# Four PSUM banks in turn for the spectral sums of an adaLN block, forward and backward

## The chip, the cores and the metric

The kernel runs on one NeuronCore of one Trainium2 chip. Its time is the device time in microseconds from launch to end. Three runs of the kernel before gave 1523.6, 1515.2 and 1520.55 us, so the median is 1520.55 us. One further execution was profiled. It took 1518.75 us, and from its first to its last instruction (the span) 1516.6 us; every duration below is from that execution.

A matmul writes its sums into PSUM, a small memory with eight banks. Each bank holds 512 fp32 values per partition, and another engine must copy ("evacuate") a bank to SBUF before it can be written anew. Which bank a group of matmuls gets therefore decides which evacuation it has to wait for.

## The reference

A transformer block with a spectral mixing layer (A) and an MLP (B) is computed, with the gradients of all its inputs but one constant; S = 2048 tokens, D = 1024, F = 3584, in bf16:

```python
def _A_ref(x, w_r, w_i):
    X = rfft2(x.astype(float32), axes=(-2, -1))
    X = X * (w_r + 1j * w_i)
    return irfft2(X, s=(S, D), axes=(-2, -1)).astype(bfloat16)

def _B_ref(x, w1, b1, w2, b2):
    h = gelu(layernorm(x) @ w1 + b1)
    return h @ w2 + b2

sa, ca, ga, sb, cb, gb = split(silu(c) @ w_mod, 6)
h = layernorm(x) * (1 + ca) + sa
x = x + ga * _A_ref(h, w_r, w_i)
h = layernorm(x) * (1 + cb) + sb
x = x + gb * _B_ref(h, w1, b1, w2, b2)
# returned: x, and the vector-Jacobian product of this block for grad_out
```

## The kernel before

The 2-D transforms are done as matmuls with cosine and sine matrices. The input is folded first (sums and differences of mirrored rows and columns), which leaves four parity classes: cosine even and odd, sine even and odd (`CE, CO, SE, SO` = 0, 1, 2, 3). One function, `spectral_core`, does the whole of it twice: forward on the normalised x, and backward on the gradient. Its steps are:

1. `s_fwd`, once for each class: the transform along the tokens. Eight groups of four matmuls 128x512 (`pu`, L470), into `ps_s` banks.
2. `pair(n, par, m)`, eight times (n = 4·par + m): the transform along the features. For t = 0 the cosine class and for t = 1 the sine class of one parity; for each t two banks `pcs[0]` and `pcs[1]`, and into each of them two groups of two matmuls 128x256 (L503). Both banks are then copied into `cs`, with `nc.any` in the forward pass (the scheduler takes ACT or DVE; the line is L641) and on ACT in the backward pass (L644). Then a chain of DVE operations follows (all through the helper `tt`, L172): `Pt` from `cs`, the products `qa` and `qb` with the spectral weights `ws`, and two rows of `R`. Forward, `Pt` is stored to `d_P`; backward it is loaded again into `pf` and gives the weights' gradients, which are stored by SP and by POOL (L549, L550). The weights of the next pair are loaded by `pair_load` (SP L488 and POOL L489, which gathers mirrored rows).
3. `s_inv`, once for each class: the inverse along the tokens from `R`, eight groups of four matmuls 128x512 (`pv`, L563), in `ps_s` banks. `CE` and `SE` run ahead of pair 6, `CO` and `SO` after pair 7.
4. The inverse along the features: for each of four blocks of tokens (i = 0 to 3) and each class, two groups of four matmuls 128x256 (`po`, L628), each copied into `ct` by ACT or DVE (L631). `consume` then works on the block: `consume_fwd` unfolds it, adds the residual, normalises it and stores it; `consume_bwd` goes on to the layer norm's gradient and the output.

PSUM is shared out by three helpers over one pool. `ps_s` has two banks in turn (tag s: `pu`, `pv`, and in the backward pass `accCA`, an accumulator held from the first block of step 4 to the last), `ps_d` two (tag d: `pcs`, `po`, and other accumulators) and `ps_f` four (tag f: the large products). A tile asked for under a tag gets the tag's next bank in turn and waits until that bank's last reader is done.

PE always has other work beside these steps. Forward, it is `pp` (L678, the gradient of the output through w2; w2's tiles are loaded by SP as `wt`, and the results stored by POOL as `d_ph`). Backward, it is `gw2acc` (L1114, the gradient of w2): `beside_bwd` puts four groups of 16 matmuls 128x512 into each pair, and their evacuations `gwo` (L1119) are stored by POOL (L1121); the operand tiles `hh` are loaded by SP (L1139, two for each pair). In step 4 `consume_bwd` places more of it, and then `gw1acc` (L1181, the gradient of w1), whose remainder runs alone at the end. Between the passes lie the MLP's products: `pz` (L795) with the GELU on ACT and DVE (L798 to L806), `pbo` (L836), and `pg` (L1020).

The order on each engine isn't the order of the text. A scheduler places every instruction when its operands and its tile's bank come free in the scheduler's own model, and takes those under `tc.high_priority()` (the evacuations) first. So a change of banks can move instructions on all engines.

Of the kernel before, what the change touches and what calls it, by code (L numbers as in the profile page):

```python
# [35 lines left out]
def kernel(  # L36
# [39 lines left out]
    def ps_d(name):  # L76
        return psum.tile([P, 512], FP32, tag="d", name=name)
# [84 lines left out]
    def w_plus(w, par, m):  # L162
        return bass.AP(tensor=w.tensor, offset=w.offset + (256 * m + par) * DF, ap=[[2 * DF, P], [1, DF]])

    def w_idx(par, m):
        return bass.IndirectOffsetOnAxis(ap=widx[:, 4 * par + m:4 * par + m + 1], axis=0)
# [4 lines left out]
    def tt(out, a, b, op):  # L171
        return nc.vector.tensor_tensor(out=out, in0=a, in1=b, op=op)  # L172
# [303 lines left out]
    def spectral_core(fwd, fb, sms, em, css, pt, evac_u, evac_c, evac_v, consume, o4tag, pfs=None, fill=lambda n: None, mid=lambda: None, beside=lambda n: None):  # L476
# [16 lines left out]
        def pair(n, par, m):  # L493
            ws = ws2[:, n % 2]
            cs = css[n % 2]
            for t in range(2):
                cl = par + 2 * t
                pcs = [ps_d("pcs"), ps_d("pcs")]
                for dc in range(4):
                    po = pcs[0 if dc < 2 else 1]  # L500
                    st = dc % 2 if dc < 2 else 3 - dc
                    for h in range(2):
                        nc.tensor.matmul(po[:, st * 256:(st + 1) * 256], lhsT=Us[cl][:, 2 * dc + h, m * P:(m + 1) * P],  # L503
                                         rhs=em[:, 2 * dc + h, :], start=(h == 0), stop=(h == 1))
                c0 = 0 if t == 0 else PW
                s0 = 1 + (PW if t == 0 else 0)
                for k, o in ((0, c0), (1, s0)):
                    with tc.high_priority():
                        evac_c(cs[:, t, o:o + 512].rearrange("p (w s) -> p s w", s=2), pcs[k].rearrange("p (s w) -> p s w", s=2))
            Pt = Pt2[:, n % 2]  # L510
            cv = cs.rearrange("p t (x w) -> p t x w", w=PW)
            tt(Pt[:, 2:0:-1, :], cv[:, 0], cv[:, 1], ALU.add)
            tt(Pt[:, 0:4:3, :], cv[:, 0], cv[:, 1], ALU.subtract)
            sp_m = par == 0 and m == 0
            if sp_m:
                nc.vector.tensor_copy(out=Pt[0:1, 0:2, :], in_=cv[0:1, 0])
                nc.vector.tensor_scalar(out=Pt[0:1, 2, :], in0=cv[0:1, 1, 0], scalar1=-1.0, scalar2=None, op0=ALU.mult)
                nc.vector.tensor_copy(out=Pt[0:1, 3, :], in_=cv[0:1, 1, 1])
            Pv = Pt.rearrange("p (s r) w -> p s r w", r=2)[:, :, :, 0:DF]
            if fwd:  # L520
                nc.gpsimd.dma_start(out=d_P[n], in_=Pt.rearrange("p a w -> p (a w)"))
            qa = qa2[:, n % 2]
            qb = qb2[:, 0]

            def bc(x):
                a = ws[:, x, :, 0:DF]
                return bass.AP(tensor=a.tensor, offset=a.offset, ap=[a.ap[0], a.ap[1], [0, 2], a.ap[2]])

            tt(qa[:, :, :, 0:DF], Pv, bc(0), ALU.mult)
            tt(qb[:, :, :, 0:DF], Pv, bc(1), ALU.mult)  # L530
            tt(qa[:, :, 0, 0:DF], qa[:, :, 0, 0:DF], qb[:, :, 1, 0:DF], ALU.add if fwd else ALU.subtract)
            tt(qa[:, :, 1, 0:DF], qa[:, :, 1, 0:DF], qb[:, :, 0, 0:DF], ALU.subtract if fwd else ALU.add)
            rc = par * 4 + m
            rs = (par + 2) * 4 + m
            tt(R[:, rc, :, 0:DF], qa[:, 0, :, 0:DF], qa[:, 1, :, 0:DF], ALU.add)
            r_in[0] = tt(R[:, rs, :, 0:DF], qa[:, 0, :, 0:DF], qa[:, 1, :, 0:DF], ALU.subtract)
            if sp_m:
                nc.vector.tensor_copy(out=R[0:1, rc, :, 0:DF], in_=qa[0:1, 0, :, 0:DF])
                nc.vector.tensor_copy(out=R[0:1, rs, :, 0:DF], in_=qa[0:1, 1, :, 0:DF])
            if not fwd:  # L540
                pf = pfs[n % 2]
                m1 = qb2[:, 0]
                m2 = qb2[:, 1]
                tt(m1[:, :, :, 0:DF], Pv, pf[:, :, :, 0:DF], ALU.mult)
                tt(m2[:, :, :, 0:DF], Pv, pf[:, :, ::-1, 0:DF], ALU.mult)
                tt(pf[:, 0, :, 0:DF], m1[:, :, 0, 0:DF], m1[:, :, 1, 0:DF], ALU.add)
                tt(pf[:, 1, :, 0:DF], m2[:, :, 0, 0:DF], m2[:, :, 1, 0:DF], ALU.subtract)
                for x, w in ((0, out_2), (1, out_3)):
                    nc.sync.dma_start(out=w_plus(w, par, m), in_=pf[:, x, 0, 0:DF])  # L549
                    nc.gpsimd.indirect_dma_start(out=w, out_offset=w_idx(par, m), in_=pf[:, x, 1, 0:DF], in_offset=None)  # L550
# [38 lines left out]
        for par in range(2):  # L589
            for m in range(4):  # L590
                if par == 1 and m == 2:
                    s_inv(CE, smis[0])
                    s_inv(SE, smis[0])
                pair(par * 4 + m, par, m)
                if par * 4 + m < 7:
                    pair_load(par * 4 + m + 1)
                beside(par * 4 + m)
                if par == 0 and m == 0:
                    load_smi()
                if par == 0 and m > 0:  # L600
                    v = 0 if fwd else 1
                    if m == 1:
                        gm = reg.tile([P, 12, 256], BF16, name="gm", tag="gm")
                        for cl in (CO, SO):
                            with tc.issue_after(ld_in[0].ins):
                                nc.sync.dma_start(out=gm[:, 2 * cl:2 * cl + 2, :], in_=d_E[:, v, 2 * cl:2 * cl + 2, :])
                    else:
                        cl = (CE, SE)[m - 2]
                        for h in range(2):
                            with tc.issue_after(ld_in[0].ins):  # L610
                                nc.sync.dma_start_transpose(out=gm[:, 2 * cl:2 * cl + 2, h * P:(h + 1) * P],
                                                            in_=d_E[:, v, 2 * cl + h, :])
# [6 lines left out]
        for i in range(4):  # L619
            o4 = ct[:, 3 * (i % 2)]  # L620
            for cl in range(4):
                for hh_ in range(2):
                    po = ps_d("po")
                    for d2 in range(2):
                        dc = 2 * hh_ + d2
                        for h in range(2):
                            gi = 2 * dc + h + (4 if (dc >= 2 and cl >= 2) else 0)
                            nc.tensor.matmul(po[:, d2 * 256:(d2 + 1) * 256], lhsT=Vs[cl][:, 2 * dc + h, i * P:(i + 1) * P],  # L628
                                             rhs=gm[:, gi, :], start=(h == 0), stop=(h == 1))
                    with tc.high_priority():  # L630
                        nc.any.tensor_copy(out=o4[:, cl, hh_ * 512:(hh_ + 1) * 512], in_=po[:])  # L631
            consume(i, o4, ct[:, 1 + i % 2], ct[:, 2 - i % 2], xts[i % 2])
# [87 lines left out]
    def consume_fwd(i, o4, tmp, tmp2, x4):  # L720
# [13 lines left out]
        nc.sync.dma_start(out=chunk_rows(d_n3, i), in_=tmp)  # L734

    spectral_core(True, fbuf, (smA, smB), em1[:, 1], [css[:, 0], css[:, 1]], new_pair_temps(PXT[2:6]),
                  act_copy, act_copy, act_copy, consume_fwd, "fr")

# [262 lines left out]
    for b in range(NB):  # L1001
# [26 lines left out]
        for i in range(4):  # L1028
            t = 4 * b + i
# [9 lines left out]
        for i in range(4):  # L1039
            t = 4 * b + i  # L1040
# [175 lines left out]
    def beside_bwd(n):  # L1216
        for k in range(4):
            fill(1)
            if 3 - k < (1, 2, 2, 2, 2, 2, 3, 3)[n]:
                with tc.issue_after(hh_in[0].ins):  # L1220
                    next(rows34)

    spectral_core(False, fbuf2, (smA2, smB2), em2, [css2[:, 0], css2[:, 1]],
                  new_pair_temps(["t0", "t1", "t2", "t3"]), act_copy, s_copy, act_copy, consume_bwd, "fr", pfs, fill, mid_bwd, beside_bwd)

# [55 lines left out]
```

## Time and profile before

| What | us |
|---|---|
| Median of three runs | 1520.55 (1515.2 to 1523.6) |
| Profiled execution | 1518.75 |
| Its span, first to last instruction | 1516.6 |
| PE busy in the span | 1413.6 (93%) |
| DVE busy | 1070.0 (71%) |
| ACT busy | 724.6 (48%) |
| Mean granted TensorE clock | 0.980 |

The stages of that span, from the busy time by window:

| Stage, us from the start | length | PE busy | DVE busy | ACT busy | clock |
|---|---|---|---|---|---|
| modulation, w2 transposes, first pp: 0 to 95 | 95 | 67.9 | 71.7 | 61.4 | 0.93 |
| forward fold and `s_fwd`: 95 to 153 | 58 | 57.1 | 28.4 | 33.4 | 1.00 |
| forward pairs: 153 to 220 | 67 | 59.1 | 53.1 | 37.3 | 0.95 |
| forward inverse: 220 to 276 | 56 | 55.0 | 41.3 | 35.8 | 1.00 |
| rest of pp: 276 to 349 | 73 | 70.8 | 67.0 | 45.4 | 1.00 |
| MLP forward: 349 to 780 | 431 | 414.3 | 325.2 | 269.1 | 1.00 |
| MLP backward, first gw2: 780 to 1067 | 287 | 263.2 | 203.4 | 82.8 | 0.96 |
| backward `s_fwd`: 1067 to 1096 | 29 | 28.8 | 0.7 | 19.6 | 1.00 |
| backward pairs: 1096 to 1252 | 156 | 144.4 | 104.7 | 52.2 | 0.97 |
| backward inverse: 1252 to 1380 | 128 | 123.3 | 100.3 | 60.7 | 1.00 |
| rest of gw1: 1380 to 1517 | 137 | 129.8 | 74.4 | 26.9 | 0.99 |

How to read such a profile: an engine's busy time says how much work it has, not whether it sets the time. That is told by what ends the idle time of each engine (the waits), and by the chain of waits, which goes back from the last instruction to whatever released it. "Clock" is the share of full speed that the chip granted to TensorE in that stretch.

The durations of the operations that the change touches, from the groups by tile: a `pcs` or `po` matmul lasts 272 ns, and since matmuls overlap, a group of four takes some 0.43 us; an evacuation of `pcs` takes 738 ns on ACT and 736 on DVE in the forward pass, and 741 on ACT in the backward pass; one of `po` 585 ns on ACT and 692 on DVE. There are 256 `pcs` and 256 `po` matmuls, and 64 evacuations of each.

### The profile page before, as it was taken

How to read it: one execution, taken by the hardware profiler on the slowest of the kernel's cores; microseconds unless marked ns; L12 is line 12 of the kernel's file. 1: busy time of each engine (PE TensorE's matmuls, PEld its weight loads, DVE VectorE, ACT ScalarE, POOL GpSimd, SP SyncE). 2: the span in 40 equal slices, each digit the busy share in tenths (PEclk: the TensorE clock that was granted, in tenths of full speed). 3: DMA queues.
4: the chain of work that ended last, by engine and by line, in shares of the span. 5: the costliest groups of instructions: out<-in, count | busy, mean ns of one | idle time of the engine just before them, and what ended most of it. 6: DMA issues, size and time to landing. Idle time of an engine off the chain costs nothing.

```text
span 1516.6 us, 18226 instructions
## 1 busy us (share of the span) xinstructions
PE 1413.6 (93%) x6702; PEld 654.1 (43%) x6835; DVE 1070.0 (71%) x1575; ACT 724.6 (48%) x959; POOL 370.1 (24%) x427
## 2 busy tenths in 40 slices
PE   5899899999899999999889999969999899999998
PEld 2444445444344444444334444424444444444443
DVE  5883767897799887877313877958075775998633
ACT  4765556758787765666011423322622344443211
POOL 5710621210112122211112101321033331232333
PEclk8999999999999999999999999979999999999999
DMA  9882564999787776899956246398388976856994
GB/s 337 260 222 70 153 181 153 277 241 323 236 251 238 231 239 230 242 291 261 326 190 220 99 150 222 124 225 195 82 202 212 238 227 177 225 170 164 274 244 151
DMA packets 358168, 324.27 MB, mean 214 GB/s; under 512 B 209191, under 2 KB 300861, under 8 KB 357824
## 3 DMA queue, kind: packets, MB, share of 16 engines
q1 hardware_dynamic: 324192, 207.71, 51.3%
q0 software_dynamic: 33888, 115.41, 22.8%
q8 instruction: 53, 0.87, 0.2%
q14 instruction: 35, 0.29, 0.1%
HBM read 164.15 MB, written 109.10 MB: 180 GB/s over the span
## 4 chain that ended last, share of the span: by engine, by line
PE 49%; DVE 20%; issue 10%; DMA 10%; ACT 6%; POOL 4%; SPq 1%; POOLq 0%; ACTq 0%; DVEq 0%
PE pbo L836 10%; PE pz L795 10%; PE gw2acc L1114 9%; PE pg L1020 5%; PE gw1acc L1181 4%; PE pv L563 3%; DVE ct L172 3%; PE pu L470 3%; PE pp L678 2%; DVE got L919 2%; DVE fbuf L172 2%; PE po L628 1%; DVE gn3a L924 1%; DMA gB<-in_grad_out_dram 1%; ACT ct L460 1%
## 5 line engine op out<-in xcount | busy, mean ns | idle before, releaser
L678 PE MATMUL pp<-gBoT,wt 128*128 128x512 bf16 x876 | 198.4, 379 | 5.6 <-DMA wt<-in_B_w_dram 1.9
L1020 PE MATMUL pg<-w1T,gzr 128*128 128x512 bf16 x876 | 195.3, 381 | 1.5 <-issue 0.7
L1181 PE MATMUL gw1acc<-gzh,n3n 128*128 128x512 bf16 x876 | 194.7, 379 | 0.9
L795 PEld LDWEIGHTS <-w 128*128 128x128 bf16 x896 | 87.7, 98 | 111.3 <-issue 7.9
L1020 PEld LDWEIGHTS <-gzr 128*128 128x128 bf16 x896 | 87.2, 98 | 109.4 <-issue 7.2
L678 PEld LDWEIGHTS <-wt 128*128 128x128 bf16 x896 | 87.4, 98 | 106.3 <-issue 3.7
L1181 PEld LDWEIGHTS <-n3n 128*128 128x128 bf16 x896 | 87.4, 98 | 104.1 <-issue 1.3
L795 PE MATMUL pz<-n3Ta,w 128*128 128x512 bf16 x437 | 99.5, 383 | 5.0 <-ACT gt L798 4.2
L1114 PE MATMUL gw2acc<-gB,hhsA 128*128 128x512 bf16 x437 | 100.7, 383 | 1.2 <-DMA hhsA<-d_hh 0.4
L1119 ACT CAST gwo<-gw2acc 128x512 bf16<-128x512 f32 x54 | 30.8, 584 | 146.7 <-PE gw2acc L1114 94.8
L795 PE MATMUL pz<-n3Tb,w 128*128 128x512 bf16 x439 | 98.4, 379 | 0.5
L836 PEld LDWEIGHTS <-hhA 128*128 128x128 bf16 x608 | 59.0, 98 | 75.2 <-issue 5.2
L798 ACT ACTIVATE gt<-pz,b_col 128x512 bf16<-128x512 f32 x112 | 73.0, 683 | 34.4 <-PE pz L795 32.3
L804 ACT ACTIVATE gt<-gt 128x2048 bf16<-128x2048 bf16 x28 | 53.5, 1910 | 67.5 <-DVE gt L172 67.5
L172 DVE TENSOR_TENSOR gt<-gt,gt 128x2048 bf16<-128x2048 bf16 x56 | 68.5, 1223 | 21.6 <-ACT gt L806 20.9
L1185 ACT CAST gwo<-gw1acc 128x512 bf16<-128x512 f32 x49 | 28.3, 582 | 104.9 <-PE gw1acc L1181 91.5
L172 DVE TENSOR_TENSOR ct<-ct 128x2048 bf16<-128x2048 bf16 x64 | 76.0, 1219 | 3.2 <-ACT ct L631 1.9
L1114 PE MATMUL gw2acc<-gB,hht 128*128 128x512 bf16 x251 | 59.4, 396 | 14.3 <-DMA hht<-d_hh 10.3
L1114 PEld LDWEIGHTS <-hhsA 128*128 128x128 bf16 x448 | 44.1, 99 | 52.6 <-issue 2.7
L800 ACT ACTIVATE gt<-gt 128x2048 bf16<-128x2048 bf16 x28 | 53.4, 1907 | 0.6
L806 ACT ACTIVATE gt<-gt 128x2048 bf16<-128x2048 bf16 x28 | 53.4, 1907 | 0.5
L958 DVE CUSTOM_DVE_ANT_0 otl<-otl 128x1024 bf16<-128x1024 bf16 x16 | 19.1, 1223 | 43.6 <-DMA otl<-in_w_mod_dram 35.6
(313 smaller groups left out, 2521.1 us busy)
## 6 DMA issues: line engine op xcount, KB each, us to landing
gzr<-d_gz SPq DMA_DIRECT2D x28, 512.0 KB
wblk<-in_w_mod_dram SPq DMA_DIRECT2D x12, 1024.0 KB
d_ph<-pho POOLq DMA_DIRECT2D x21, 512.0 KB
out_dram<-otl POOLq DMA_DIRECT2D x40, 256.0 KB
d_hh<-hhA POOLq DMA_DIRECT2D x19, 512.0 KB
w2sD<-in_B_w_dram SPq DMA_DIRECT2D x14, 512.0 KB
hhC<-d_ph SPq DMA_DIRECT2D x14, 512.0 KB
w2sA<-d_ph SPq DMA_DIRECT2D x14, 512.0 KB
```

What stands on the lines that cost most here:

```text
L172: return nc.vector.tensor_tensor(out=out, in0=a, in1=b, op=op)
L470: last_pu[0] = nc.tensor.matmul(pu[:], lhsT=fb[:, i, cl, c8 * P:(c8 + 1) * P], rhs=sm[:, i, :], start=(i == 0), stop=(i == 3))
L678: last_pe[0] = nc.tensor.matmul(pp[:], lhsT=wt[:, fg % 2, cch, k * P:(k + 1) * P], rhs=gBoT[j][:, cch, :], start=(cch == 0), stop=(cch == ...
L795: last_pe[0] = nc.tensor.matmul(pz[:], lhsT=w1s[g][:, cch, k * P:(k + 1) * P], rhs=n3T[:, cch, :], start=(cch == 0), stop=(cch == NDC - 1))
L798: nc.scalar.activation(out=zb[:, k, :], in_=pz[:], func=ACT.Identity, bias=b1_col[:, fc:fc + 1], scale=1.0)
L800: nc.scalar.activation(out=av, in_=zb, func=ACT.Square)
L804: nc.scalar.activation(out=sg, in_=bv, func=ACT.Sigmoid, scale=2.0 * GK)
L806: nc.scalar.activation(out=bv, in_=bv, func=ACT.Sigmoid, scale=-2.0 * GK)
L836: last_pe[0] = nc.tensor.matmul(pbs[i][:], lhsT=hh[:, k, i * P:(i + 1) * P], rhs=wp[:, k, :], start=False, stop=(g == 6 and k == 3))
L1020: nc.tensor.matmul(pgs[i][:], lhsT=gzt[g][:, k, i * P:(i + 1) * P], rhs=w1Ts[g][:, k, h * KH:(h + 1) * KH], start=(g == 0 and k == 0), sto ...
L1114: nc.tensor.matmul(acc[:], lhsT=hh_s[hh_o[fc]][:, t, :], rhs=gBs[t // 4][:, t % 4, h * KH:(h + 1) * KH], start=(t == 0), stop=(t == NT - 1))
L1181: nc.tensor.matmul(acc[:], lhsT=n3ns[t // 4][:, t % 4, cch * P:(cch + 1) * P], rhs=gz2[t // 8][:, t % 8, :], start=(t == 0), stop=(t == NT ...
```

## The change

Two lines are changed, both in `spectral_core`, so both passes are concerned. In `pair`, the two sums of t = 0 stay in the d banks, and the two of t = 1 take the s banks. In step 4, the first half of each class (`hh_` = 0) stays in a d bank and the second takes an s bank. The matmuls, the copies and all sizes are as before; so are the other users of the banks.

```diff
             for t in range(2):
                 cl = par + 2 * t
-                pcs = [ps_d("pcs"), ps_d("pcs")]
+                pcs = [(ps_d, ps_s)[t]("pcs") for _ in range(2)]
                 for dc in range(4):
                     po = pcs[0 if dc < 2 else 1]
...
             for cl in range(4):
                 for hh_ in range(2):
-                    po = ps_d("po")
+                    po = (ps_d, ps_s)[hh_]("po")
                     for d2 in range(2):
                         dc = 2 * hh_ + d2
```

## The prediction

> **What bounds the kernel now.** I read the page first (busy shares, slices, chain), then the waits of the two spectral passes, the busy time by stage, and the timelines of PE and ACT at the one place that decides.
>
> ```profile
> PE 1413.6 (93%) x6702; PEld 654.1 (43%) x6835; DVE 1070.0 (71%) x1575; ACT 724.6 (48%) x959; POOL 370.1 (24%) x427
> PEclk8999999999999999999999999979999999999999
> PE 49%; DVE 20%; issue 10%; DMA 10%; ACT 6%; POOL 4%; SPq 1%; POOLq 0%; ACTq 0%; DVEq 0%
> ```
>
> PE is busy for 1413.6 of 1516.6 us, so everything that a PSUM change could win lies in 103 us of PE idleness, in the clock lost after idle stretches, and only where PE sets the pace. The chain of waits is half PE and otherwise DVE, DMA and issue: in some stages PE waits because data are late, and banks don't help there. The waits from 1096 to 1380 us, the whole backward pass of the changed lines, name the PSUM waits:
>
> ```profile
> PE pcs L503 <- ACT cs01b L644: 8.6, 8, 2.5
> PE po L628 <- ACT ct L631: 3.8, 3, 2.7
> PE pv L563 <- ACT V L641: 1.6, 1, 1.6
> PE gw2acc L1114 <- DMA hhsA<-d_hh: 0.4, 1, 0.4
> ```
>
> So 8.6 us are lost at the second half of the sums (t=1) until ACT has read the first half's two banks, in eight waits: five of 0.22 to 0.27 us and three long ones, 2.51 us at 1163.81, 2.31 at 1184.30, 2.50 at 1236.36. The inverse sums lose 3.8 us. The forward pass (150 to 280 us) shows far less of it:
>
> ```profile
> PE pv L563 <- DVE R L172: 5.4, 1, 5.4
> ...
> PE pcs L503 <- ACT cs L641: 1.3, 6, 0.4
> ```
>
> There PE's one large wait is for DVE's product R, which no bank shortens. By stage (window: length, busy time of PE, PEld, DVE, ACT, POOL, then the granted clock, DMA share, GB/s), pairs 4, 5, 6 and 7 of the backward pass:
>
> ```profile
> 1160.00:1180.70 20.70, 17.69 (x80) 8.17 (x80) 11.16 (x17) 4.75 (x8) 7.03 (x9) 0.92 0.96 206
> 1180.70:1201.00 20.30, 17.57 (x80) 8.19 (x81) 12.15 (x18) 4.76 (x8) 6.75 (x8) 0.92 0.98 222
> ...
> 1216.50:1232.60 16.10, 15.77 (x79) 7.81 (x80) 10.35 (x14) 6.76 (x9) 4.12 (x5) 1.00 0.78 245
> 1232.60:1252.50 19.90, 17.35 (x80) 8.42 (x80) 15.60 (x24) 7.55 (x13) 5.34 (x8) 0.91 0.82 240
> ```
>
> A pair with a long wait takes 19.9 to 20.7 us, one without 16.1: each wait of some 2.5 us costs about 4, since the granted clock after it is lower (0.91 to 0.92 over the pair). PE at pair 7, and ACT just then:
>
> ```profile
> 1232.61 1.04 PE L503 MATMUL pcs<-empf,U 128*128 128x256 bf16 x8
> 1233.48 0.38 PE L1114 MATMUL gw2acc<-gB,otl 128*128 128x512 bf16 x1
> 1236.36 1.72 PE L503 MATMUL pcs<-empf,U 128*128 128x256 bf16 x8 [2.50 <-ACT cs01b L644]
> ```
>
> ```profile
> 1232.99 1.24 ACT L460 ACTIVATE xt<-xt,stats 128x1024 bf16<-128x1024 bf16 x1
> 1234.13 1.55 ACT L1119 CAST gwo<-gw2acc 128x512 bf16<-128x512 f32 x3
> 1235.55 1.36 ACT L644 CAST cs01b<-pcs 128x512 bf16<-128x512 f32 x2
> ```
>
> Eight matmuls take 1.72 us after the wait instead of 1.04. ACT reads the sums at 1235.55 only because three gw2 casts and a scale stand ahead; those are late because the stores of gwo are (ACT waits 39.2 us for them between 1160 and 1253).
>
> **The change, part by part.** Instruction counts stay; one evacuation moves from ACT to DVE. The t=1 sums get the two class-sum banks (tag s), the inverse sums alternate between d and s. By the built order of both programs, the four sums of a pair now run back to back (16 groups in a row for the forward pairs 0 to 3), and the gw2acc or pp matmul that stood between the halves follows.
>
> *Backward pairs 0 to 5 (0 us).* Their waits are 0.22+0.27+0.27+0.27+2.51+2.31 = 5.85 us, with the clock some (20.70−16.10)+(20.30−16.10)+1.03 = 9.8 us. But pairs 3 to 5 are held by the transfers: SP's loop of loads for one pair has a period of about 20 us (1140.96, 1159.97, 1180.45, 1200.68), the DMA share is 0.96 to 0.98, PE already waits 0.43 us for a tile of hhsA at 1173.83 that lands just then, and at 1204.42 PE waits 1.59 us for ACT, itself behind a gwo store until 1202.81. A PE that arrives earlier waits longer there. Price if that cover is gone: 9.8 us.
>
> *Backward pairs 6 and 7 (−4.5 us).* Here tiles are ahead. Pair 6's wait gives 0.2. In pair 7 four groups (4×0.43=1.7 us) and 64 gw2acc matmuls (64×0.216=13.85) from 1232.6 end at 1248.2 instead of 1252.5, where pv needs R. DVE's last R ended at 1247.3 after a start set by the fourth evacuation (1238.85); ACT would have that about 0.4 earlier: R at 1246.9, in time. So −4.3, of which 2.5 is the wait and the rest clock and issue. DVE then idles 16.59 us until po, so the consume chain moves with it.
>
> [...]
>
> *Backward inverse sums (0 us).* Waits now: 0.91+0.15 in the second block, 2.69+0.19 in the third. The accumulator accCA (column sums for the gradient of ca) holds one s bank from the first block to the last, so blocks 1 to 3 have three banks, not four. The long wait is ACT behind a scale (L923) that waits 4.11 us for DVE; a third bank buys one group, about 0.5 us. Against it, one evacuation in block 1 now stands on ACT behind a scale that waits for its load, about 0.5. Bounds: −3.9 (all four gone) to +2.7 (another wait of the longest kind).
>
> *Forward (0 us).* The pcs waits (1.3 for ACT, 0.4 for DVE) go, and 17 pp matmuls (17×0.216=3.7 us) move ahead of the 5.41 us wait; but that wait ends with R, and R with the weight load, whose GpSimd step took 11.26 us at 168.37 while VectorE ran products without a break. The next sync, PE's 4.17 us wait on ACT's GELU at 409.69, closes a chain of DVE, ACT and stores (294 to 409) in which PE work doesn't count. Against it: DVE takes five more pcs evacuations (0.74 each) in the pair chain and one pv evacuation between two R rows, which I estimate to hold PE 2.3 us. DVE waits 2.77, 3.07, 2.13, 2.55 and 11.93 us in these 130 us, which covers most. On SP the load of w2 tiles for group 6 is now ahead of two weight loads, on POOL one d_ph store ahead of a weight load; each can hold a pair by a few us. Bounds: −4 (the 3.7) to +6 (2.3+3.7).
>
> Sum: 0−4.5+0+0 = −4.5, so 1518.75−4.5 = 1514.3 beside the profiled run. That run lies 1.8 below the median of the three (1520.55; 1515.2 to 1523.6): against the median 1516.
>
> **The rivals.**
> - *A, all PE waits are recovered.* For: PE is on the chain in the passes, and an earlier PE may also bring gwo stores forward. Against: the 20 us loop. 9.8+4.5+3.9 = 18.2 us: 1502.
> - *B, slower: the forward chain moves out.* Place: DVE and the weight loads of pairs 3 to 6 (180 to 237 us). From the point where the six DVE evacuations and a delayed load exceed the waits of 2 to 3 us that each pair has, R, pv, po and the consume chain move one to one until 409. Price: 6×0.74 = 4.4, the 2.3 at pv, and a weight load later by one store of d_P (5.5 as it took at 181.45): 12 in full, less the 4.3 won later, +8: 1528.5. For: every step of 294 to 409 is DVE, ACT or a store. Against: 11.93 us of DVE idleness just before po.
> - *C, nothing: what is saved is waited for elsewhere,* also in pair 7, if pv waits there for R or smB. 1520. [...]
>
> **How the numbers follow.** The forecast has 0.35, A 0.19, B 0.33, C 0.13. About 0.5% (7.6 us) is what a measurement here can tell from no change. Faster by more: most of A (0.18) and the forecast's best part, where some of the 9.8 us comes too (0.10): 0.28. Slower by more: B where its price isn't offset (0.29). The rest, 0.43, is within. The range for 8 in 10 reaches into A and B: 1506 to 1530; the likeliest case's own is 1512 to 1519.
>
> **What would show it.** Right: in the backward pass no wait of pcs on cs01b above 0.3 us, the clock of pair 7 back to 1.00 and its period near 16; pairs 4 and 5 still near 20, with more waiting for hhsA or at pv; PE's wait on GELU near 409 as before. Wrong: pairs 4 and 5 at 16 us (A); the first unfold of the forward pass (237.56) or the first pz wait later by over 4 us (B); a long wait of pv for R after pair 7 (C); po waits above 3 us in blocks 1 to 3.

## The result and the profile after

The changed kernel takes 1510.4 us (median of 22 runs, 1499.97 to 1522.62), the kernel before 1520.95 us in its 22 runs beside it. The ratio is 0.9921, with a 95% interval of 0.9904 to 0.9938: some 12 us faster. (It leaves out one slow run of the changed kernel, 1522.62 us; the medians of all runs, slow one included, differ by 10.6 us.) The forecast was 1516, within 1506 to 1530; so the time lies in the range, but the gain is more than twice the 4.5 us that the sum gave.

The profiled execution's span went from 1516.6 to 1505.0 us. Its page, busy time by engine and granted clock by slice:

```profile
span 1505.0 us, 18218 instructions
...
PE 1408.0 (94%) x6703; PEld 655.0 (44%) x6835; DVE 1068.8 (71%) x1574; ACT 721.4 (48%) x960; POOL 371.6 (25%) x427
...
PEclk8999999999999999999999999989999999999999
```

PE's busy time fell by 5.6 us with the same matmuls. In pairs 4, 5 and 7 alone it fell by 5.8, where the clock went from 0.91 and 0.92 to 1.00: that is slow clock that is gone. Over the whole span the mean clock is no higher (0.978, before 0.980): the first 95 us, which the change doesn't touch, ran at 0.89 instead of 0.93, and the backward inverse at 0.97 instead of 1.00. The waits of PE in the backward pass of the changed lines (1080 to 1400 us) answer to the four lines shown before:

```profile
PE po L628 <- DVE ct L631: 6.5, 2, 4.5
PE pv L563 <- ACT V L641: 2.3, 1, 2.3
PE po L628 <- ACT ct L631: 1.0, 1, 1.0
PE gw2acc L1114 <- DMA otl<-d_hh: 0.8, 1, 0.8
PE gw2acc L1114 <- DMA hhsA<-d_hh: 0.4, 1, 0.4
```

The wait of pcs on cs01b, 8.6 us before, is gone entirely; the waits of the inverse sums rose from 4.0 to 7.5 us. By stage, pairs 4, 5, 6 and 7 (columns as before: window, its length, busy time of PE, PEld, DVE, ACT, POOL, then the clock, DMA share and GB/s), and last the first pv pass, between pairs 5 and 6:

```profile
1153.10:1169.20 16.10, 15.64 (x80) 7.73 (x80) 12.87 (x19) 4.60 (x8) 7.73 (x8) 1.00 0.94 257
1169.20:1185.70 16.50, 15.61 (x79) 7.74 (x80) 11.00 (x17) 4.60 (x8) 7.39 (x7) 1.00 1.12 235
1203.70:1219.20 15.50, 15.39 (x79) 7.82 (x80) 10.41 (x14) 6.68 (x9) 3.58 (x3) 1.00 0.76 234
1219.20:1234.80 15.60, 15.55 (x81) 7.81 (x80) 15.17 (x24) 6.71 (x11) 5.65 (x8) 1.00 0.88 228
1185.77:1203.70 17.93, 15.62 (x65) 6.71 (x65) 12.61 (x18) 9.66 (x17) 8.58 (x9) 0.90 0.93 268
```

Pairs 4 and 5, 20.7 and 20.3 us before, now take 16.1 and 16.5 at full clock, although the DMA engines are as full as they were (share 0.94 and 1.12, before 0.96 and 0.98). PE's timeline at pair 4 shows why, with ACT's beside it:

```profile
1153.11 1.91 PE L503 MATMUL pcs<-empf,U 128*128 128x256 bf16 x16
1154.86 7.07 PE L1114 MATMUL gw2acc<-gB,otl 128*128 128x512 bf16 x31
1162.33 7.08 PE L1114 MATMUL gw2acc<-gB,hhsA 128*128 128x512 bf16 x32 [0.40 <-DMA hhsA<-d_hh]
```

```profile
1154.66 1.07 ACT L1119 CAST gwo<-gw2acc 128x512 bf16<-128x512 f32 x2 [7.62 <-PE pcs L503]
1155.62 2.57 ACT L644 CAST cs01b<-pcs 128x512 bf16<-128x512 f32 x4
```

ACT is still late: it reads the first sum only at 1155.62, 2.5 us after PE began the pair (3.0 before, at 1163.01), behind the same two gw2 casts. (Their wait is put down to pcs, the last event by the profile; at this place before it was a gwo store.) But PE has by then done all four groups and is at gw2acc. ACT reads the four banks in one go, done at 1158.2, and PE needs none of them before pair 5 begins at 1169.25.

Put between marks that both programs share, the 11.6 us of the two spans are:

| Stretch | before, us | after, us | difference |
|---|---|---|---|
| start to first backward pcs | 1095.47 | 1090.87 | −4.60 |
| backward pairs and first pv pass, to the second pv pass | 157.04 | 143.95 | −13.09 |
| second pv pass | 13.81 | 13.81 | 0 |
| inverse sums, first to last | 112.68 | 117.94 | +5.26 |
| rest | 137.60 | 138.43 | +0.83 |

Three questions follow. Why did the pairs win 13 us instead of 4.5? Are the 4.6 us ahead of them the forward pass's? And are the 5.3 us given back the price of the inverse sums' edit?

### The profile page after: what moved, and what is told of

It reads as the page before. It is cut to its first block, busy times and chain, and to the rows that moved or that the text cites. A ratio compares the mean times of both kernels' runs of the same rounds, so it can differ in the third digit from the quotient of the medians.

```text
span 1505.0 us, 18218 instructions
## 1 busy us (share of the span) xinstructions
PE 1408.0 (94%) x6703; PEld 655.0 (44%) x6835; DVE 1068.8 (71%) x1574; ACT 721.4 (48%) x960; POOL 371.6 (25%) x427
## 4 chain that ended last, share of the span: by engine, by line
PE 42%; DVE 19%; DMA 8%; issue 6%; ACT 5%; POOL 1%; SPq 0%; POOLq 0%; DVEq 0%; ACTq 0%
PE pbo L836 10%; PE pz L795 10%; PE gw2acc L1114 8%; PE gw1acc L1181 4%; PE pg L1020 4%; DVE ct L172 4%; DVE got L919 2%; PE pu L470 2%; PE pv L563 2%; ACT ct L460 1%; DVE gn3a L924 1%; DVE st L436 1%; DMA gB<-in_grad_out_dram 1%; DMA n3u<-d_n 1%; DMA w2sA<-in_B_w_dram 1%
## 5 line engine op out<-in xcount | busy, mean ns | idle before, releaser
L1186 POOL DMA_DIRECT2D out_dram<-gwo x56 | 30.5, 546 | 84.5 <-ACT gwo L1185 74.3
```

## The experiments

All ratios are to the kernel before, run on the same chip at the same time, with a 95% interval.

**The t=1 sums in the backward pass alone.**

```diff
-                pcs = [ps_d("pcs"), ps_d("pcs")]
+                pcs = [(ps_d, ps_d if fwd else ps_s)[t]("pcs") for _ in range(2)]
```

> Only the t=1 sums of the backward pass take the class-sum banks; the forward pass and all inverse sums stay on two banks. Theory P (PE paces the pairs, and SP's loop of loads only followed it): no wait of pcs on cs01b above 0.3 us, pairs 0 to 7 at 15.6 to 16.2 us each, the stretch from the first backward pcs to the second pv pass 144 us instead of 157, and since the po waits stay at about 4 us, the whole is 13 us faster than before (ratio 0.991 to 0.992). Rival L (the transfers hold pairs 3 to 5, as the prediction had it): pairs 4 and 5 stay at 19 to 20 us with the waits moved to hhsA or pv, some 4.5 us faster (0.997). Rival E (the pairs were only faster because of the other order ahead of them): this kernel's pairs stay as before, no gain.

Measured: 0.9921 (0.9892 to 0.9950), the ratio of the whole change. PE's three largest waits from 1070 to 1400 us:

```profile
PE po L628 <- ACT ct L631: 5.0, 2, 4.1
PE pv L563 <- ACT V L641: 1.8, 1, 1.8
PE gw2acc L1114 <- DMA hhsA<-d_hh: 0.8, 1, 0.8
```

No wait of pcs is left; pairs 4 and 5 take 16.5 and 16.1 us, and the stretch of the pairs 142.3 us. Theory P is right and rival L wrong; rival E falls too, since the forward pass is unchanged here. The po waits are 5.2 us and not the 4 that P named, although the inverse sums have their two banks.

**The t=1 sums in both passes, the inverse sums as before.** The first line of the diff alone.

> The t=1 sums take the class-sum banks in both passes; the inverse sums stay on two banks. If the inverse sums' alternation is what gave back some 4 to 6 us at 1280 to 1366 us in the changed kernel (9 us of DVE waiting for one evacuation, 7.5 us of PE waiting), this one keeps the whole 13 us of the pairs: po waits of about 4 us as before, 14 to 17 us faster than before (ratio 0.989 to 0.991), so 3 to 6 faster than the changed kernel. If the giving back came with the earlier arrival at these blocks alone (loads of x late whatever the banks), it stays: about 10 us faster (0.993).

Measured: 0.9891 (0.9852 to 0.9931). The pairs take 144.0 us, the inverse sums' stretch 115.6 with 5.8 us of po waits. The ratio is the expected one, but its interval takes in that of the whole change, so the times don't tell the two kernels apart; and the waits didn't fall to 4.

**The inverse sums alone.** The second line of the diff alone.

> Only the inverse sums alternate between the banks, in both passes; pcs stays on two. If the alternation itself costs: backward pairs as before (pcs waits 8.6 us in all), po waits of some 7 us instead of 4, up to 4 us slower than before (ratio 1.000 to 1.003). If it is free or helps and the loss came with the earlier arrival: po waits below 4 us, 0 to 3 us faster (0.998 to 1.000).

Measured: 1.0008 (0.9983 to 1.0033): no difference. The pcs waits are there (7.0 us; pairs 156.3 us), the po waits are 5.2 us, between the two expectations, and the inverse sums' stretch 114.7.

**Both edits in the forward pass alone.**

> Both edits in the forward pass alone, the backward pass as before. If the 2.3 us at the first long wait for GELU (409.69 before, 407.39 after) are the forward pass's own and last to the end: 2 to 3 us faster (ratio 0.998 to 0.999), with that wait ending near 407.4 again. If they were luck of one execution: no difference (1.000). The backward pairs keep their 8.6 us of waits in either case.

Measured: 0.9992 (0.9964 to 1.0019). The long wait for GELU ended at 407.58, as in the changed kernel (407.39; before 409.69). But a gain of 2 us at that point can't be told from none in the whole. The backward pairs keep their waits (8.9 us) and take 157.0 us.

**Three banks.** In the backward pass only the first t=1 sum is given a class-sum bank:

```diff
-                pcs = [ps_d("pcs"), ps_d("pcs")]
+                pcs = [(ps_d, ps_d if fwd else ps_s)[t]("pcs"), ps_d("pcs")]
```

> Backward pass only, and only the first of the two t=1 sums takes a class-sum bank, the second takes the d bank of the first t=0 sum again: three banks. Theory P (what counts is how much work PE can do before it needs an evacuation: one more group of 0.43 us with three banks, all of a pair's 64 gw2acc matmuls, 13.8 us, with four): the five short waits of 0.22 to 0.27 us go, the long ones shrink by 0.4 us each but stay near 2 us with their slow clock; 1 to 4 us faster than before (ratio 0.9975 to 0.9995). Rival (any further bank breaks the coupling, or the contiguous order is what helps): long waits gone, 0.991 to 0.993 as with four.

Measured: 0.9958 (0.9934 to 0.9982), so about half of the gain. The middle value is more than P named, though the interval reaches into P's range. In the pairs' stretch (153.3 us) it is clearly less than with four banks. PE's timeline at pairs 4 and 7:

```profile
1153.86 1.47 PE L503 MATMUL pcs<-empf,U 128*128 128x256 bf16 x12
1157.20 0.60 PE L503 MATMUL pcs<-empf,U 128*128 128x256 bf16 x4 [1.88 <-ACT cs01b L644]
1157.64 7.07 PE L1114 MATMUL gw2acc<-gB,otl 128*128 128x512 bf16 x31
...
1220.05 1.47 PE L503 MATMUL pcs<-empf,U 128*128 128x256 bf16 x12
1227.27 1.01 PE L503 MATMUL pcs<-empf,U 128*128 128x256 bf16 x4 [5.74 <-ACT cs01b L644]
1228.08 9.26 PE L1114 MATMUL gw2acc<-gB,otl 128*128 128x512 bf16 x31
```

The wait is where P put it: three groups run, the fourth waits. What P missed is the clock. After 1.88 us the next 31 matmuls take 7.07 us, full speed (clock 1.00 over that pair); after 5.74 they take 9.26 (0.86 from 1220 to 1244). So pair 4 costs its wait and no more, where 2.5 us had cost 4. The long wait of pair 7 did not shrink but grew, from 2.50 to 5.74 us.

**The stores of gwo on ACT, two banks.** This is a test of why ACT is late:

```diff
         if h == 1:
-            nc.gpsimd.dma_start(out=out_6[fc * P:(fc + 1) * P, :], in_=gwo[:, fc % 2])
+            nc.scalar.dma_start(out=out_6[fc * P:(fc + 1) * P, :], in_=gwo[:, fc % 2])
```

> Two banks as before; the stores of gwo are issued by ACT right behind their evacuations instead of by POOL, so no longer behind POOL's other stores. PE's order in the pairs is as before. If POOL's queue makes those stores late, these hold ACT, and ACT's lateness makes the long pcs waits: ACT's waits for gwo stores fall from 44 us to under 15, the long waits in pairs 4 and 5 go, the one in pair 7 (ACT behind an x load) stays; 7 to 10 us faster than before (ratio 0.993 to 0.996). If the stores are late because the DMA engines are full: the waits and the pairs stay as they are, and ACT's own issues cost up to 3 us (1.000 to 1.002).

Measured: 1.0028 (1.0004 to 1.0052), slower by a little. PE's waits from 1070 to 1420 us:

```profile
PE pv L563 <- DVE V L641: 9.7, 1, 9.7
PE gw2acc L1114 <- DMA otl<-d_hh: 5.6, 1, 5.6
...
PE pcs L503 <- ACT cs01b L644: 1.8, 8, 0.2
```

All eight pcs waits fell to 0.2 us without any further bank, the one of pair 7 too, which was expected to stay. The list of ACT's waits no longer names gwo stores (44.1 us before). But ACT wasn't set free, as its timeline at pair 5 shows (ACTq is ACT issuing the store):

```profile
1175.30 1.35 ACT L644 CAST cs01b<-pcs 128x512 bf16<-128x512 f32 x2
1189.59 0.34 ACTq L1121 DMA_DIRECT2D out_dram<-gwo  x1
1189.97 1.33 ACT L644 CAST cs01b<-pcs 128x512 bf16<-128x512 f32 x2 [13.32 <-DMA otl<-d_hh]
```

Seven such stretches, each ending with the issue of a store, come to some 40 us; the list puts them down to loads and another store, the last events by the profile. What changed for PE is the order: the first two copies of a pair now stand ahead of the wait, where in the kernel before the gw2 casts that waited stood ahead of them (at 1162.05, the copies at 1163.01). So the test shows that the pcs waits hang on what stands before the copies in ACT's order. Why the stores are held, POOL's queue or the transfers, it doesn't settle. The time went elsewhere. The scheduler now put one evacuation of V on DVE, and DVE had to get through modulation rows first, which waited for their loads:

```profile
1190.90 1.22 DVE L958 CUSTOM_DVE_ANT_0 otl<-otl 128x1024 bf16<-128x1024 bf16 x1 [8.77 <-DMA otl<-d_gmod]
...
1207.16 1.23 DVE L958 CUSTOM_DVE_ANT_0 otl<-otl 128x1024 bf16<-128x1024 bf16 x1 [3.07 <-DMA otl<-in_w_mod_dram]
...
1210.25 0.68 DVE L641 CAST V<-pv 128x512 bf16<-128x512 f32 x1
```

**The same, with V's backward evacuations kept on ACT.**

> Two banks as before, gwo stores issued by ACT, and the backward evacuations of V kept on ACT (in the run with ACT's stores alone one of them had gone to DVE, behind modulation rows that waited for a load, and PE waited 9.7 us for it). If the eight pcs waits, all 0.2 us there, are worth what four banks are worth: pairs at 16.1 us, no wait of pv for V above 3 us, 8 to 12 us faster than ACT's stores alone, 4 to 9 faster than before (ratio 0.994 to 0.997). If the earlier stores delay the loads of hh and of the modulation rows by as much as the pcs waits were: waits of PE for hh tiles of 5 us and more stay, 0.998 to 1.003.

Measured: 0.9973 (0.9943 to 1.0002), between the two expectations. The first five pairs run at 16.1 us each, with pcs waits of 0.2. But PE then waits 8.0 us for V all the same, because ACT, done with a gwo cast at 1198.0, gets to issue that store only at 1203.61 and reads V after it. Moving the stores trades one wait for another; the banks remove one and add none of that size.

**The stores on ACT, with the pcs line.**

> The pcs line in both passes, the inverse sums on two banks, and the gwo stores issued by ACT. If four banks already cover ACT's lateness in the pairs, only the wait of pv for ACT's evacuation of V (2.6 us with the pcs line alone) can still go: the pairs stay at 15.6 us and the whole is 0 to 4 us faster than the pcs line alone (ratio 0.987 to 0.989). If the store's place matters beyond the pairs, or costs ACT, it shows as more than 4 us faster or as slower than 0.990.

Measured: 0.9997 (0.9974 to 1.0020): the whole gain is lost. PE waits 11.8 us for V on DVE and 9.7 us for hh tiles, and the pairs' stretch is 167.2 us. The expectation's second case is what happened: the stores' place isn't harmless even where the banks cover ACT's lateness at the sums.

**The last evacuation of the first backward po block on DVE.** In the changed kernel that block ended as follows (ACT, then DVE, then PE at the second block):

```profile
1255.49 1.24 ACT L460 ACTIVATE xt<-xt,stats 128x1024 bf16<-128x1024 bf16 x1 [3.84 <-DMA xt<-in_A_x_dram,xu]
1256.64 0.56 ACT L631 CAST ct<-po 128x512 bf16<-128x512 f32 x1
```

```profile
1257.23 9.55 DVE L172 TENSOR_TENSOR ct<-ct 128x2048 bf16<-128x2048 bf16 x8 [4.49 <-ACT ct L631]
```

```profile
1286.35 3.31 PE L628 MATMUL po<-gm,V 128*128 128x256 bf16 x16 [4.47 <-DVE ct L631]
```

One evacuation stands behind a scale that waits for its load, DVE's unfolding starts 4.5 us late, and PE waits 4.5 us one block on. The edit moves that evacuation and nothing else on PE:

```diff
-                        nc.any.tensor_copy(...)
+                        (nc.any if fwd or i > 0 or cl < 3 or hh_ == 0 else nc.vector).tensor_copy(...)
```

> Both edits, and the last evacuation of the first backward po block is taken by DVE instead of ACT, where it stood behind a scale that waited for its x load. PE's order is that of the changed kernel, instruction by instruction. If that one evacuation is what gives time back: DVE's wait of 4.5 us ahead of the unfolding goes, PE's wait of 4.5 us ahead of the second po block falls below 1.5, and the kernel is 3 to 5 us faster than the changed one (ratio to before 0.989 to 0.990). If PE's arrival at the second block is early in any case: the wait stays above 3 us and the ratio stays at 0.992.

Measured: 0.9911 (0.9876 to 0.9945), not to be told from the change. PE at the second and third blocks:

```profile
1282.89 2.09 PE L628 MATMUL po<-gm,V 128*128 128x256 bf16 x16 [0.67 <-DVE ct L631]
...
1320.28 3.63 PE L628 MATMUL po<-gm,V 128*128 128x256 bf16 x16 [5.28 <-ACT ct L631]
```

The wait at the second block fell to 0.67 as expected, and one of 5.28 us stood at the third. The cause of the wait at the second block was right and the gain wasn't there: a wait moved on. In this profile PE also waited 4.3 us for hh tiles in pairs 3 to 5.

**More PE work ahead of the po blocks.** Three kernels with `fill((7, 7, 8, 8)[i])` for `fill((6, 6, 8, 8)[i])`: with the pcs line, with nothing else, and with both edits.

> The pcs line in both passes, the inverse sums on two banks, and one more piece of 16 matmuls (3.5 us) placed ahead of each of the backward po blocks 1 and 2 (fill 7, 7, 8, 8 instead of 6, 6, 8, 8); the pure gw1acc tail is shorter by as much. If the po waits come from PE reaching these blocks before DVE and ACT are through with the block before, whatever the banks: the po waits in 1280 to 1370 us fall from 5 to 8 us to under 2 us, 3 to 6 us faster than the pcs line alone (ratio to before 0.985 to 0.988). If the waits only move on, to block 3 or to the tail: 0.989 to 0.991.

> The kernel before with nothing but that fill (7, 7, 8, 8). Same theory: the po waits (3.9 us before) fall under 1 us, the pcs waits stay at about 8.6 us; 2 to 4 us faster than before (ratio 0.997 to 0.999). If the waits move on: 1.000.

> Both edits and that fill. If the alternation of the inverse sums matters only through PE's early arrival, this one equals the pcs line with the fill: ratio 0.985 to 0.988, po waits under 2 us. If three banks let PE run into waits of their own (accCA holds a class-sum bank): po waits of 3 us or more stay, 0.989 to 0.992.

Measured: 0.9885 (0.9861 to 0.9910), 0.9996 (0.9972 to 1.0020) and 0.9912 (0.9882 to 0.9943). None differs from its kernel without the fill. With the pcs line the two po waits were:

```profile
1329.95 1.03 PE L628 MATMUL po<-gm,V 128*128 128x256 bf16 x8 [3.99 <-DVE ct L631]
...
1373.34 1.03 PE L628 MATMUL po<-gm,V 128*128 128x256 bf16 x8 [2.25 <-DVE ct L631]
```

Again no wait at the second block, and waits at the third and the fourth instead. With the fill alone they were 0.24, 3.35 and 1.47 us at these three blocks. With both edits one was left, 4.06 at the fourth, but PE then waited 5.3 us more for DVE at gw1acc; that profile is of the slowest of its seven runs. So PE coming later took the wait from one block and put it into a later one, without a gain, and the theory that PE is simply early falls. A reading that fits these rows is that the evacuations of po have places in DVE's and ACT's order behind the block before, and that those engines get to them when that block's chain is through; no run tests it alone.

Over the eleven profiles in which POOL stores gwo, the stretch of the backward pairs sorts by the banks, whatever else was edited (with the stores on ACT it was 165.4 and 155.1 us with two banks and 167.2 with four, so there it doesn't):

| Banks of the backward pcs | kernels (profiles) | pairs' stretch, us |
|---|---|---|
| two | before, inverse sums alone, forward alone, fill alone | 157.0, 156.3, 157.0, 158.2 |
| three | three banks | 153.3 |
| four | the change, backward alone, pcs alone, last po on DVE, two with fill | 144.0, 142.3, 144.0, 146.0, 140.8, 143.2 |

## Why the prediction came out as it did

- **What bounds the kernel: right.** The waits of pcs on cs01b were what the change removed; neither the forward half of the change nor the inverse sums' line moved the time by itself.
- **Backward pairs 0 to 5, "0 us": the step that failed, the cover by the transfers.** I held that "pairs 3 to 5 are held by the transfers", with SP's loop of some 20 us as the ground, and gave 9.8 us as the price if that cover is gone. From the first pcs to the first pv the profiles went from 105.5 to 94.9 us: 10.6 won. SP's loop had been long because PE was; in the changed kernel it starts at 1134.31, 1153.34, 1169.10, 1187.70 and 1203.14, 17.2 us apart on average. PE's waits for hh tiles there came to 1.2 us, so the transfers held PE by that much and no more. The same kernel with one evacuation moved had 1.9 and 2.1 us of them in pairs 4 and 5, and its pairs' stretch was 146.0 us.
- **Backward pairs 6 and 7, "−4.5": right in mechanism, mis-sized in the sum.** Pair 7 went from 19.90 to 15.56 us (−4.3, as forecast), pair 6 gave 0.55 instead of 0.2. But the first pv pass between them took 17.93 us instead of 15.56: ACT is still held by a gwo store there (a wait of 2.26 us, before 1.59), and the clock was 0.90. In all −2.5 in this execution. The prediction had named this wait, under the pairs before it, as one that an earlier PE makes longer; it did, and with the clock took back 2.4 us.
- **Inverse sums, "0" with bounds −3.9 to +2.7: +5.3 in this profile, past the bound; by the times none is shown.** The evacuation behind the x load was named, at "about 0.5"; the wait behind it was 4.5. But their stretch took 112.7 to 116.4 us in the five profiles with the old code there and gwo on POOL (before, backward alone, pcs alone, forward alone, three banks), and 114.7 with the inverse sums alone. The profile of before was the shortest of all. The edit's own ratio is 1.0008 (0.9983 to 1.0033). Beside four pcs banks the kernels without it came to 0.9921, 0.9891 and 0.9885, those with it to 0.9921, 0.9911 and 0.9912: whether it costs 2 or 3 us there stays open.
- **Forward, "0": borne out.** 0.9992 (0.9964 to 1.0019). R, pv and po did come later (the first unfolding at 238.96 instead of 237.56), DVE took six more pcs evacuations (nine instead of three) where five were named, the pv evacuation on DVE didn't hold PE, since DVE was there first and waited 2.1 us for it, and the GELU wait ended 2.3 us earlier after all. Rival B's mechanism was seen, at 1.4 us instead of 12, and closed up behind. The 4.6 us ahead of the first backward pcs mean nothing: in six kernels whose forward pass isn't edited that mark lies between 1090.8 and 1097.2, in the eight others between 1086.5 and 1104.8.
- **The rivals.** A was right for the pairs and priced them at 14.3 us (9.8 and 4.5; measured 13.1); it expected 3.9 more from the inverse sums, which didn't come. C's case at pair 7 was not seen; of what was won, the first pv pass took back the 2.4 us above. Two of the prediction's own signs of being wrong came: pairs 4 and 5 at 16 us, which it had given to A, and a po wait above 3 us (4.47 at the second block).
- **The number.** That 1510.4 lies within the range is not the sum's merit. The range had been drawn to reach into A, and A is what the pairs did; the sum itself, with the transfers as cover, was 1516.

With the failed term put right the sum is −9.8−4.5 = −14.3. The pairs' stretch gave −13.1 in the profile, and the whole, by the times, −12 (1520.95 less 0.79%).

## What to carry to other kernels

Where PE waits for the reader of a PSUM bank, ask how much work PE has from the last free bank to the next need: here a third bank covered one group of 0.43 us, the fourth let PE go on to 13.8 us of other work, and the reader's lateness, uncured, cost nothing any more at these sums. A transfer loop as long as PE's period proves nothing about who sets the pace; see whether the loop waits for what PE frees, and give the case that PE leads as much chance as the other. Where several engines hand work on in a fixed order, a wait removed in one block came back in the next (4.5 us at one block, 5.3 at the following one), so a wait is worth its length only where what follows it isn't held by the same chain.

## What was not expected of the hardware

In these runs the clock after a wait didn't go by the wait's length alone. After waits of PE of 1.06, 1.88 and 1.94 us for cs01b in pairs 4 and 5 the matmuls behind them ran at full speed (clock 1.00 over the pairs with the first two, with three banks; 30 matmuls of 512 columns in 6.64 us after the 1.94, with the fill alone). After waits of 2.51 us in the kernel before and 2.25 with the forward half alone, both in pair 4, the 30 behind them took 8.54, which is 1.9 more (clock 0.92 and 0.91 over the pair). Yet in pair 5 of that last kernel the 30 took 6.64 after a wait of 2.51. Between 2.1 and 2.6 us both are seen: with three banks 55 pv matmuls took 12.25 us after a wait of 2.13, and with the last po on DVE 31 of gw2acc took 8.77 after 2.14, where 31 at full speed take 7.07. The first pv pass in the changed kernel, and in the kernel with the pcs line and the fill:

```profile
1189.92 13.94 PE L563 MATMUL pv<-smi,R 128*128 128x512 bf16 x55 [2.26 <-ACT V L641]
```

```profile
1196.42 12.25 PE L563 MATMUL pv<-smi,R 128*128 128x512 bf16 x55 [2.54 <-ACT V L641]
```

The same 55 matmuls take 13.94 us after a wait of 2.26, and 12.25 after the longer one of 2.54. So a wait of this size cost its length here, or its length and nearly 2 us more, and its length doesn't tell which; no run shows what does.
